# The softmax over positions in compensated fp32: one polynomial step made plain, and the reciprocal of the rational's denominator from two exponentials

## The chip, the cores and the metric

The kernel runs on one core of a Trainium2 chip. The metric is the device time of that core in microseconds (us): 1050.5 us for the kernel before, the median of three runs (1049.24, 1050.5 and 1057.09). The profile and the trace used below are of one further execution of 1053.18 us, whose span from the first to the last instruction is 1051.3 us at a mean granted TensorE clock of 0.805 of full speed. The engines are named as in the profile: PE (TensorE matmul), PEld (its weight load), DVE (VectorE), ACT (ScalarE), POOL (GpSimd) and SP (SyncE, which only issues DMA here).

## The reference

Two blocks follow each other. The first is an attention over 32 learned memory slots: `phi` is turned into weights by a softmax over the 576 positions, keys and values are pooled with these weights, and each query attends to the 32 pooled slots.

```python
# q, k, v: (8, 8, 576, 64); phi: (8, 8, 576, 32)
a = phi - np.max(phi, axis=2, keepdims=True)
a = np.exp(a)
a = a / (np.sum(a, axis=2, keepdims=True) + 1e-09)      # softmax over the positions
k_m = np.einsum('bhsm,bhsd->bhmd', a, k)
v_m = np.einsum('bhsm,bhsd->bhmd', a, v)
scores = scale * np.matmul(q, k_m.transpose(0, 1, 3, 2))
...                                                     # softmax over the 32 slots
out = np.matmul(attn, v_m)                              # -> x: (8, 576, 512)
```

The second is a mixture of depths: in each batch the 128 rows with the highest score `x @ w_gate` are replaced by `x + g * (relu(x @ w1) @ w2)`, where `g` is the sigmoid of the score; all other rows pass through.

```python
top_idx = np.argpartition(-scores[b], capacity)[:capacity]
xe = x[b, top_idx]
ye = np.maximum(xe @ w1, 0.0) @ w2
out[b, top_idx] = x[b, top_idx] + g[:, None] * ye
```

Which rows are chosen depends on the last bits of the scores. So the kernel computes the first softmax and the pooled values very close to fp32 rounding, in many VectorE steps.

## The kernel before, in words

**The work.** There are 16 *groups*: 8 batches times 2 halves of 4 heads. The phi of a group is one tile of 128 partitions (4 heads x 32 slots) by 576 positions. `softmax(i, ch)` turns it into weights, `keys(i, ch)` transposes them on PE, pools the keys and writes the weights in two parts (high and low bits) to DRAM. `split_v` splits the values into two parts and writes them to DRAM too. `values(st)` reads both back for two batches at a time and pools the values with 2304 small matmuls (L371). `attention(b)` is the second softmax, the output rows, the gate's scores, the ranking and the gather of the chosen rows; `ffn(b, t)` is the two-layer network on these rows.

**The softmax of a group.** All tiles are 128x576. The exponential is range reduced, exp(r) 2^q, and exp(r) is a rational: a numerator polynomial `num` with coefficients EXP_P and a denominator `den` with EXP_Q. Most Horner steps are done by `fma` (L216 to L225): six VectorE operations that multiply a value `val` by `r` with compensation, from its coarse part `h` (an int16 tile that ScalarE rounds, "vh" or "dh") and the coarse and fine parts `rh`, `rl` of `r`. It runs once for `den` (L229) and three times for `num` (L234 to L243). Then the quotient num/den is formed: `y0` is a first quotient in whole steps of a grid (an int16 tile from ScalarE's Exp, L233), `num - y0*den` is the remainder (L246 to L253), the reciprocal of `den` comes from a product of terms of ScalarE's Square (`sq` at L242, `s2` at L249, with L247 between them), and L257 to L259 multiply the remainder by it and add `y0`. L262 multiplies by 2^q and sums over the positions; L265 to L276 divide by the sum with compensation. ScalarE's part of all this goes through the helper `act` (L176).

**The order of the work.** The kernel schedules by hand. Every job is a generator, and the main loop (L747 on) is a list of *turns*: each turn takes one step of one softmax, some steps of `values`, one step of each live attention and two steps of the ffn queue. So a `yield` in `softmax` is a turn in which the other jobs get their share:

```python
if working and next(working[0], working) is working: ...     # one step of a softmax
if len(working) == 2 and turn % 2:
    next(working[1], None)                                    # split_v, every other turn
for _ in range(steps()):                                      # 7, 10 or 12 steps of values
    next(sums, None)
if attend_all is None and set(order[1]) <= set(made):
    finish(working.pop(1))                                    # what is left of split_v, at once
    ...                                                       # pools of the attention take its place
```

A softmax with its keys is 11 turns. Groups 0 to 7 are handled in two chains, `ex0` and `ex1`, whose steps alternate. When the odd groups are made, the pools of the second chain and of `split_v` are given up for the attention's tiles; groups 8 to 15 go through one chain, with the attentions between their steps. Each engine executes its own instructions in the order in which they were issued here.

Of the kernel before, what the change touches and what calls it, by code (L numbers as in the profile page):

```python
# [8 lines left out]
F32 = mybir.dt.float32  # L9
# [5 lines left out]
AF = mybir.ActivationFunctionType  # L15
ALU = mybir.AluOpType
# [8 lines left out]

LOG2E = 1.44269504088896341
LN2_HI, LN2_LO = 6.93145752e-1, 1.42860677e-6
EXP_P = (1.0, 7.257664613233124478488e-01, 2.473615434895520810817e-01,  # L30
         5.114512081637298353406e-02, 6.757896990527504603057e-03, 5.082762527590693718096e-04)
EXP_Q = (1.0, -2.742335390411667452936e-01, 2.159509375685829852307e-02)
EXP_LOWEST = -87.0
Y0_SCALE = 12 * 0.6931471805599453


@with_exitstack
def kernel(
# [61 lines left out]
    def load_k(i, ch):  # L100
        ks[i] = exs[ch].tile([PT, NC, D // NG], F32, name="kb")
        nc.sync.dma_start(out=ks[i], in_=k[groups[i]])
# [60 lines left out]
    def constant(value):  # L163
        t = const.tile([P, 1], F32, name=f"c{len(biases)}")
        nc.gpsimd.memset(t, value)
        return t


    UP, GRID = 2.0 ** 23, 2.0 ** -11
    biases = {}  # L170
    for x in (EXP_P[3] * UP, EXP_P[4] * UP, EXP_P[3] * UP * GRID, EXP_Q[1] * UP,
              EXP_Q[1] * UP * GRID, 127 * UP, -1.5, Y0_SCALE):
        biases[x] = constant(x)

    def act(dst, src, s=1.0, c=0.0, func=AF.Identity):
        nc.scalar.activation(dst, src, func, bias=biases[c] if c else 0.0, scale=s)  # L176

    tt, stt = nc.vector.tensor_tensor, nc.vector.scalar_tensor_tensor
# [3 lines left out]
    def softmax(i, ch):  # L182

        ex = exs[ch]

        def t(name, dtype=F32):

            return ex.tile([P, NC * P if name in WIDE else S], dtype, name=name)[:, :S]

        r = phis.pop(i)  # L190
        mx = ex.tile([P, 1], F32, name="mx")
        nc.vector.tensor_scalar(out=t("num"), in0=r, scalar1=1.0, scalar2=None, op0=ALU.mult,
                                op1=ALU.max, accum_out=mx)
        nc.vector.tensor_scalar(out=r, in0=r, scalar1=mx, scalar2=EXP_LOWEST,
                                op0=ALU.subtract, op1=ALU.max)
        q = t("q", I16)
        act(q, r, LOG2E)
        yield
        for ln2 in (LN2_HI, LN2_LO):
            stt(out=r, in0=q, scalar=-ln2, in1=r, op0=ALU.mult, op1=ALU.add)  # L200

        rh, rl = t("rh", I16), t("rl")
        act(rh, r, 2.0 ** 11)
        num, den = t("num"), t("den")
        act(num, r, EXP_P[5] * UP, EXP_P[4] * UP)
        dh = t("dh", I16)
        act(dh, r, EXP_Q[2] * UP * GRID, EXP_Q[1] * UP * GRID)
        act(den, r, EXP_Q[2] * UP, EXP_Q[1] * UP)
        yield
        tt(out=num, in0=num, in1=r, op=ALU.mult)  # L210
        vh = t("vh", I16)
        act(vh, num, GRID, EXP_P[3] * UP * GRID)
        act(num, num, 1.0, EXP_P[3] * UP)
        stt(out=rl, in0=rh, scalar=-GRID, in1=r, op0=ALU.mult, op1=ALU.add)

        def fma(val, h, c):  # L216


            lo, big, low = t("lo"), t("big"), t("low")
            stt(out=lo, in0=val, scalar=GRID, in1=h, op0=ALU.mult, op1=ALU.subtract)  # L220
            tt(out=lo, in0=lo, in1=rh, op=ALU.mult)  # L221
            tt(out=big, in0=h, in1=rh, op=ALU.mult)
            tt(out=low, in0=val, in1=rl, op=ALU.mult)
            tt(out=low, in0=low, in1=lo, op=ALU.add)  # L224
            stt(out=val, in0=big, scalar=c * UP, in1=low, op0=ALU.add, op1=ALU.add)  # L225

        yield
        load_k(i, ch)
        fma(den, dh, EXP_Q[0])  # L229
        dh = t("dh", I16)  # L230
        act(dh, den, GRID / 2)
        y0 = t("y0", I16)
        act(y0, r, 1.0, Y0_SCALE, AF.Exp)  # L233
        for c in (EXP_P[2], EXP_P[1], EXP_P[0]):  # L234
            yield
            fma(num, vh, c)
            if c != EXP_P[0]:
                vh = t("vh", I16)
                act(vh, num, GRID)
            if c == EXP_P[2]:  # L240
                sq = t("rl2")
                act(sq, den, 1.0 / UP, -1.5, AF.Square)  # L242


        dl, p = t("lo"), t("big")
        stt(out=dl, in0=den, scalar=GRID / 2, in1=dh, op0=ALU.mult, op1=ALU.subtract)  # L246
        stt(out=p, in0=sq, scalar=0.75, in1=den, op0=ALU.add, op1=ALU.mult)  # L247
        s2 = t("low")
        act(s2, p, 1.0 / UP, -1.5, AF.Square)  # L249
        tt(out=p, in0=y0, in1=dh, op=ALU.mult)  # L250
        tt(out=num, in0=num, in1=p, op=ALU.subtract)
        tt(out=dl, in0=y0, in1=dl, op=ALU.mult)
        tt(out=num, in0=num, in1=dl, op=ALU.subtract)  # L253
        two_q = t("den", I32)
        yield
        act(two_q, q, UP, 127 * UP)
        stt(out=num, in0=s2, scalar=0.75, in1=num, op0=ALU.add, op1=ALU.mult)  # L257
        stt(out=num, in0=sq, scalar=0.75, in1=num, op0=ALU.add, op1=ALU.mult)
        stt(out=num, in0=num, scalar=GRID, in1=y0, op0=ALU.mult, op1=ALU.add)  # L259
        sm = ex.tile([P, 4], F32, name="sm")  # L260
        e = t("e")
        stt(out=e, in0=num, scalar=GRID / 2, in1=two_q.bitcast(F32),  # L262
            op0=ALU.mult, op1=ALU.mult, accum_out=sm[:, 0:1])

        nc.vector.tensor_scalar_add(sm[:, 0:1], sm[:, 0:1], 1e-9)  # L265
        nc.vector.reciprocal(sm[:, 1:2], sm[:, 0:1])
        nc.vector.tensor_single_scalar(sm[:, 2:3].bitcast(I32), sm[:, 0:1].bitcast(I32), -4096,
                                       op=ALU.bitwise_and)
        nc.vector.tensor_sub(sm[:, 3:4], sm[:, 2:3], sm[:, 0:1])
        nc.vector.tensor_scalar_mul(sm[:, 2:3], sm[:, 2:3], -1.0)  # L270
        a0 = t("vh", F16)
        nc.scalar.activation(a0, e, AF.Copy, scale=sm[:, 1:2])
        yield
        for part in (2, 3):
            stt(out=e, in0=a0, scalar=sm[:, part:part + 1], in1=e, op0=ALU.mult, op1=ALU.add)
        stt(out=e, in0=e, scalar=sm[:, 1:2], in1=a0, op0=ALU.mult, op1=ALU.add)  # L276
        soft[i] = e
        yield
        yield from keys(i, ch)
# [28 lines left out]
    def keys(i, ch):  # L308
        ex, (b, g) = exs[ch], groups[i]
        a = soft.pop(i)  # L310
        kb = ks.pop(i)
        aS = ex.tile([P, NC * P], F32, name="lo")[:PT].rearrange("p (c m) -> p c m", m=P)
        for c0 in range(0, NC, 3):
            tp = bank([PT, 3, P])
            for c in range(3):
                nc.tensor.transpose(out=tp[:, c], in_=a[:, (c0 + c) * PT:(c0 + c + 1) * PT],  # L316
                                    identity=ident)
            nc.scalar.activation(aS[:, c0:c0 + 3], tp, AF.Copy)  # L318
        yield
        hi = ex.tile([P, NC * P], F32, name="big")[:PT].rearrange("p (c m) -> p c m", m=P)  # L320
        lo = ex.tile([P, NC * P], F32, name="low")[:PT].rearrange("p (c m) -> p c m", m=P)
        nc.vector.tensor_single_scalar(hi.bitcast(I32), aS.bitcast(I32), -4096,
                                       op=ALU.bitwise_and)
        nc.vector.tensor_sub(lo, aS, hi)  # L324
        for part, src in enumerate((lo, hi)):
            for h in range(4):
                nc.gpsimd.dma_start(  # L327
                    out=aparts[h, b, g, part].rearrange("(c p) m -> p c m", p=PT),
                    in_=src[:, :, h * M:(h + 1) * M])
        km = bank([P, 2, 2 * M])  # L330
        for rr in range(2):
            for c in range(NC):
                nc.tensor.matmul(out=km[:, rr], lhsT=kb[:, c, rr * P:(rr + 1) * P],  # L333
                                 rhs=aS[:, c, rr * 2 * M:(rr + 1) * 2 * M],
                                 start=(c == 0), stop=(c == NC - 1))
        for u in range(2):
            part = slice(u * Dh, (u + 1) * Dh)
            nc.scalar.activation(kbd[b][part, 2 * g:2 * g + 2, u * M:(u + 1) * M],
                                 km[part, :, u * M:(u + 1) * M], AF.Copy)
# [407 lines left out]
    while True:  # L747
# [27 lines left out]
        for _ in range(2):  # L775
# [8 lines left out]
                            op0=ALU.mult, op1=ALU.add)  # L784
# [42 lines left out]
```

## Time and profile before

| Stretch (us from the start) | What runs | DVE busy | PE busy | ACT busy | DMA share |
|---|---|---|---|---|---|
| 0 to 326.6 | groups 0 to 7 in two chains, splitting of v, values of the first two batches | 295.3 | 94.4 | 93.0 | 0.65 |
| 326.6 to 792 | groups 8 to 15 in one chain, attentions 0 to 3, values of batches 2 to 5 | 384.4 | 292.8 | 147.0 | 0.19 to 0.60 |
| 792 to 1051.3 | values of the last two batches, attentions 4 to 7, most of the ffns | 104.7 | 211.6 | 53.7 | 0.20 to 0.53 |

The stretches are cut at the start of a group's first VectorE instruction (L192; group 0 at 3.7, group 8 at 326.6, group 15 at 741.5) and shortly after the last instruction of the last softmax (L276, at 789.7). Each busy time is the sum of the durations on that engine within the stretch; a stretch in which an engine is busy nearly all of the time is bound by it. The busy times of the second and third stretch are sums over the groups' stretches of the same view.

Instructions of the softmax on 128x576 elements take close to the same time whatever they are: 742 to 885 ns on VectorE by the means of their groups, 681 to 776 ns on ScalarE. ScalarE loads its function tables once in the whole run (1283 ns).

### The profile page before, as it was taken

How to read it: one execution, taken by the hardware profiler on the slowest of the kernel's cores; microseconds unless marked ns; L12 is line 12 of the kernel's file. 1: busy time of each engine (PE TensorE's matmuls, PEld its weight loads, DVE VectorE, ACT ScalarE, POOL GpSimd, SP SyncE). 2: the span in 40 equal slices, each digit the busy share in tenths (PEclk: the TensorE clock that was granted, in tenths of full speed). 3: DMA queues.
4: the chain of work that ended last, by engine and by line, in shares of the span. 5: the costliest groups of instructions: out<-in, count | busy, mean ns of one | idle time of the engine just before them, and what ended most of it. 6: DMA issues, size and time to landing. Idle time of an engine off the chain costs nothing. (4 is left out here: it accounts for less than half of the span.)

```text
span 1051.3 us, 25384 instructions
## 1 busy us (share of the span) xinstructions
PE 598.7 (57%) x10738; PEld 439.8 (42%) x10738; DVE 784.4 (75%) x1342; ACT 293.6 (28%) x578; POOL 224.3 (21%) x335
## 2 busy tenths in 40 slices
PE   0021022255554355675567397875738969889795
PEld 0021022154443354554434374664415657544542
DVE  7899999899899968698786968698993336324940
ACT  2233233233233232323224342141432101213230
POOL 7030221220230230404113021402503011011110
PEclk9999999995665656877678699566866986989688
DMA  9364544677887825554613256463404466522320
GB/s 291 126 232 153 188 157 169 192 230 277 264 274 253 313 46 155 152 179 145 214 51 106 72 141 206 127 194 115 114 0 116 153 218 189 163 66 66 120 70 23
DMA packets 60714, 166.11 MB, mean 158 GB/s; under 512 B 10801, under 2 KB 21041, under 8 KB 60593
## 3 DMA queue, kind: packets, MB, share of 16 engines
q1 hardware_dynamic: 39088, 94.14, 29.5%
q0 software_dynamic: 21504, 70.27, 19.7%
q8 instruction: 87, 1.43, 0.6%
q14 instruction: 35, 0.28, 0.1%
HBM read 96.21 MB, written 68.16 MB: 156 GB/s over the span
## 5 line engine op out<-in xcount | busy, mean ns | idle before, releaser
L371 PE MATMUL acc<-a_rows,v_rows 32*64 32x128 f32 x9216 | 217.8, 257 | 106.7 <-DMA a_rows<-aparts 97.6
L371 PEld LDWEIGHTS acc<-a_rows,v_rows 32*64 32x64 f32 x9216 | 197.7, 167 | 150.2 <-issue 113.9
L316 PE MATMUL bank<-ident,e 128*96 128x128 f32 x96 | 22.5, 403 | 214.8 <-DVE e L276 204.6
L316 PEld LDWEIGHTS bank<-ident,e 128*96 128x96 f32 x96 | 16.0, 185 | 219.7 <-issue 183.4
L333 PE MATMUL bank<-lo,kb 96*128 96x64 f32 x384 | 67.0, 353 | 7.6 <-ACT lo L318 6.8
L333 PEld LDWEIGHTS bank<-lo,kb 96*128 96x128 f32 x384 | 65.5, 267 | 12.1 <-ACT lo L318 8.6
L327 POOL DMA_DIRECT2D aparts<-low x64 | 47.2, 746 | 104.5 <-DVE low L324 100.8
L646 PE MATMUL bank<-w_sb,hT 128*128 128x512 f32 x128 | 67.2, 661 | 0.0
L636 PE MATMUL bank<-w_sb,xeT 128*128 128x512 f32 x128 | 65.5, 647 | 2.9 <-ACT xeT L627 2.9
L530 PE MATMUL bank<-vbd,eT 128*128 128x256 f32 x160 | 60.0, 510 | 0.0
L221 DVE TENSOR_TENSOR lo<-lo,rh 128x576 f32<-128x576 f32 x64 | 56.7, 885 | 2.2
L176 ACT ACTIVATE vh<-num 128x576 int16<-128x576 f32 x32 | 21.8, 683 | 127.3 <-DVE num L225 116.7
L534 DVE TENSOR_TENSOR xj<-bank,rd 128x512 f32<-128x512 f32 x40 | 27.5, 688 | 36.8 <-PE bank L530 34.9
L537 POOL TENSOR_TENSOR xj<-xj,mean 128x1024 f32<-128x1024 f32 (+1 forms) x12 | 26.1, 2174 | 128.5 <-DVE xj L534 89.8
L583 DVE SCALAR_TENSOR_TENSOR cmp<-row,tg,wide 128x576 bf16<-128x576 f32 x40 | 32.5, 811 | 25.9 <-ACT row L569 25.1
L298 POOL DMA_DIRECT2D vparts<-vb x16 | 11.6, 726 | 186.2 <-DVE vb L295 161.9
L224 DVE TENSOR_TENSOR low<-low,lo 128x576 f32<-128x576 f32 x64 | 48.5, 758 | 2.2
L327 POOL DMA_DIRECT2D aparts<-big x64 | 46.7, 738 | 0.0
L220 DVE SCALAR_TENSOR_TENSOR lo<-num,vh 128x576 f32<-128x576 f32 x48 | 36.0, 751 | 13.2 <-ACT vh L176 13.2
L530 PEld LDWEIGHTS bank<-vbd,eT 128*128 128x128 f32 x160 | 35.0, 243 | 23.8 <-issue 19.6
L602 PE MATMUL bank<-tg,pick 128*128 128x2 f32 (+1 forms) x80 | 16.9, 329 | 47.4 <-DVE pick L597 20.2
L176 ACT ACTIVATE low<-big,c 128x576 f32<-128x576 f32 x16 | 12.4, 775 | 96.4 <-DVE big L247 96.4
(150 smaller groups left out, 1244.2 us busy)
## 6 DMA issues: line engine op xcount, KB each, us to landing
v_rows<-vparts SPq DMA_DIRECT2D x128, 288.0 KB
vparts<-vb POOLq DMA_DIRECT2D x16, 1152.0 KB, 5.2
vparts<-vhi POOLq DMA_DIRECT2D x16, 1152.0 KB, 8.9
a_rows<-aparts SPq DMA_DIRECT2D x512, 36.0 KB
vb<-in_v SPq DMA_DIRECT2D x16, 576.0 KB
kb<-in_k SPq DMA_DIRECT2D x16, 576.0 KB
qb<-in_qT SPq DMA_DIRECT2D x16, 576.0 KB
out<-xj POOLq DMA_DIRECT2D x16, 512.0 KB, 3.8
```

The costliest lines, as they stand in the source:

```text
L176: nc.scalar.activation(dst, src, func, bias=biases[c] if c else 0.0, scale=s)
L220: stt(out=lo, in0=val, scalar=GRID, in1=h, op0=ALU.mult, op1=ALU.subtract)
L221: tt(out=lo, in0=lo, in1=rh, op=ALU.mult)
L224: tt(out=low, in0=low, in1=lo, op=ALU.add)
L316: nc.tensor.transpose(out=tp[:, c], in_=a[:, (c0 + c) * PT:(c0 + c + 1) * PT], identity=ident)
L327: nc.gpsimd.dma_start(out=aparts[h, b, g, part].rearrange("(c p) m -> p c m", p=PT), in_=src[:, :, h * M:(h + 1) * M])
L333: nc.tensor.matmul(out=km[:, rr], lhsT=kb[:, c, rr * P:(rr + 1) * P], rhs=aS[:, c, rr * 2 * M:(rr + 1) * 2 * M], start=(c == 0), stop=(c = ...
L371: nc.tensor.matmul(out=accs[i][:Dh, :P].rearrange("p (h m) -> p h m", m=M), lhsT=vr[p, s], rhs=ar[p, :, s], start=(ch == 0 and s == 0), st ...
L530: nc.tensor.matmul(out=o[:, g * 4 * Dh:(g + 1) * 4 * Dh], lhsT=eT[:, g, (c0 + c) * P:(c0 + c + 1) * P], rhs=vbd[b % 3][:, g], start=False, ...
L583: nc.vector.scalar_tensor_tensor(out=cmp, in0=row, scalar=g, in1=wide[:, off:off + S], op0=ALU.is_equal, op1=ALU.mult, accum_out=equal[:, ...
L636: nc.tensor.matmul(out=ps[:n], lhsT=xeT[:, d, :n], rhs=w1_sb[:, d, f0:f0 + 512], start=(d == 0), stop=(d == KD - 1))
L646: nc.tensor.matmul(out=ps[:n], lhsT=hT[:, f, :n], rhs=w2_sb[:, f], start=(f == 0), stop=(f == KF - 1))
```

## The change

It shortens the arithmetic of `softmax` in three ways.

- One of the three compensated steps of the numerator becomes a plain fp32 one: a single multiply-add on VectorE in place of the six operations of `fma` and one rounding on ScalarE. The following coefficients move down by one.
- The reciprocal of the denominator is no longer built from two Squares and products on VectorE. ScalarE forms it straight from `r` as exp(exp(a r + b) + c), in two Exp instructions.
- `y0` is on a grid of 14 bits rather than 12, so that the remainder is smaller and needs a reciprocal of less accuracy. Two scalar_tensor_tensor that applied the two factors become one tensor_tensor, and the scaling by the grid moves into the last step.

Besides, the product `low` is the first operation of `fma` rather than the fourth, and a softmax has one `yield` less.

```diff
+INV = (0.11678339169584792, 0.8537669889679409, -2.34847734)
+LN2 = 0.6931471805599453
...
-    UP, GRID = 2.0 ** 23, 2.0 ** -11
+    UP, GRID, FINE = 2.0 ** 23, 2.0 ** -11, 2.0 ** -14
...
         tt(out=num, in0=num, in1=r, op=ALU.mult)
+        stt(out=num, in0=num, scalar=EXP_P[3] * UP, in1=r, op0=ALU.add, op1=ALU.mult)
         vh = t("vh", I16)
-        act(vh, num, GRID, EXP_P[3] * UP * GRID)
-        act(num, num, 1.0, EXP_P[3] * UP)
+        act(vh, num, GRID, EXP_P[2] * UP * GRID)
+        act(num, num, 1.0, EXP_P[2] * UP)
...
             lo, big, low = t("lo"), t("big"), t("low")
+            tt(out=low, in0=val, in1=rl, op=ALU.mult)
             stt(out=lo, in0=val, scalar=GRID, in1=h, op0=ALU.mult, op1=ALU.subtract)
             tt(out=lo, in0=lo, in1=rh, op=ALU.mult)
             tt(out=big, in0=h, in1=rh, op=ALU.mult)
-            tt(out=low, in0=val, in1=rl, op=ALU.mult)
             tt(out=low, in0=low, in1=lo, op=ALU.add)
...
-        act(dh, den, GRID / 2)
+        act(dh, den, FINE)
         y0 = t("y0", I16)
-        act(y0, r, 1.0, Y0_SCALE, AF.Exp)
-        for c in (EXP_P[2], EXP_P[1], EXP_P[0]):
+        act(y0, r, 1.0, 14 * LN2, AF.Exp)
+        inv = t("rl2")
+        act(inv, r, INV[0], INV[1], AF.Exp)
+        act(inv, inv, 1.0, INV[2] - 9 * LN2, AF.Exp)
+        for c in (EXP_P[1], EXP_P[0]):
             yield
             fma(num, vh, c)
             if c != EXP_P[0]:
                 vh = t("vh", I16)
                 act(vh, num, GRID)
-            if c == EXP_P[2]:
-                sq = t("rl2")
-                act(sq, den, 1.0 / UP, -1.5, AF.Square)
...
-        stt(out=dl, in0=den, scalar=GRID / 2, in1=dh, op0=ALU.mult, op1=ALU.subtract)
-        stt(out=p, in0=sq, scalar=0.75, in1=den, op0=ALU.add, op1=ALU.mult)
-        s2 = t("low")
-        act(s2, p, 1.0 / UP, -1.5, AF.Square)
+        stt(out=dl, in0=den, scalar=FINE, in1=dh, op0=ALU.mult, op1=ALU.subtract)
         tt(out=p, in0=y0, in1=dh, op=ALU.mult)
...
-        stt(out=num, in0=s2, scalar=0.75, in1=num, op0=ALU.add, op1=ALU.mult)
-        stt(out=num, in0=sq, scalar=0.75, in1=num, op0=ALU.add, op1=ALU.mult)
-        stt(out=num, in0=num, scalar=GRID, in1=y0, op0=ALU.mult, op1=ALU.add)
+        tt(out=num, in0=num, in1=inv, op=ALU.mult)
+        tt(out=num, in0=num, in1=y0, op=ALU.add)
...
-        stt(out=e, in0=num, scalar=GRID / 2, in1=two_q.bitcast(F32),
+        stt(out=e, in0=num, scalar=FINE, in1=two_q.bitcast(F32),
             op0=ALU.mult, op1=ALU.mult, accum_out=sm[:, 0:1])
```

## Prediction

> **What bounds the kernel now.** I read first the busy shares over time, then the busy times cut at the groups' starts, then VectorE's waits, then single instructions. The page's line of totals and three of its rows over 40 slices of 26.3 us:
>
> ```profile
> PE 598.7 (57%) x10738; PEld 439.8 (42%) x10738; DVE 784.4 (75%) x1342; ACT 293.6 (28%) x578; POOL 224.3 (21%) x335
> ...
> PE   0021022255554355675567397875738969889795
> DVE  7899999899899968698786968698993336324940
> DMA  9364544677887825554613256463404466522320
> ```
>
> VectorE's 75% is no average of alike stages: it is at 8 to 9 tenths up to slice 13, then mixed 6 to 9 up to slice 30, then 2 to 4 while PE takes over with 7 to 9. So there are three stages with different bounds, which the busy times in the stretches confirm (columns: stretch, length, busy us of PE, PEld, DVE, ACT, POOL, granted clock, DMA share, GB/s):
>
> ```profile
> 0.00:326.60 326.60, 94.36 (x2118) 86.99 (x2122) 295.30 (x429) 92.96 (x148) 78.80 (x133) 0.89 0.65 217
> ...
> 490.70:557.60 66.90, 43.56 (x779) 33.51 (x779) 55.27 (x102) 19.07 (x42) 16.82 (x21) 0.74 0.42 132
> ...
> 936.00:1051.30 115.30, 90.89 (x327) 48.45 (x326) 53.78 (x125) 29.91 (x73) 16.49 (x30) 0.84 0.20 66
> ```
>
> In the first stage DVE is busy 295 of 327 us and nothing else exceeds a third, except the DMA share of 0.65. In the second, 326.6 to 792 (eight such group stretches), DVE is busy 384 of 465 us (83%) and PE 293. In the tail, 792 to 1051, PE is busy 212 of 259 us. VectorE's waits over the whole run tell which of its gaps belong to the code that changes (columns: us in total, times, longest):
>
> ```profile
> DVE big L250 <- ACT low L176: 13.5, 16, 0.8
> DVE lo L220 <- ACT vh L176: 13.2, 18, 0.8
> DVE num L210 <- ACT num L176: 9.7, 5, 4.0
> ```
>
> The first two are small, but they recur in every group and both are of the changed code; up to 370 us all of its waits together are 25 us, 19.3 of them these two. Last, the order in time of one numerator step (start, us):
>
> ```profile
> 346.97 0.75 DVE L220 SCALAR_TENSOR_TENSOR lo<-num,vh 128x576 f32<-128x576 f32 x1
> ...
> 350.68 0.76 DVE L225 SCALAR_TENSOR_TENSOR num<-big,low 128x576 f32<-128x576 f32 x1
> 352.19 0.76 DVE L220 SCALAR_TENSOR_TENSOR lo<-num,vh 128x576 f32<-128x576 f32 x1 [0.75 <-ACT vh L176]
> ```
>
> One `fma` is 4.4 us of instructions, set 0.67 to 0.79 us apart from start to start, plus 0.8 us of waiting for ScalarE's rounding where nothing of another job stands between.
>
> **What the Trainium skill says.** "VectorE: DVE Perf Modes", section on the TRN2 errata, gives (N+151)/0.96 ns for an fp32 tensor_tensor: 757 ns at N = 576. The trace has 750 to 758, so no form in the diff is cheaper than another and only the count matters. "ScalarE: Activation LUTs", "What ACT_TABLE_LOAD costs", gives 280 + 0.833 N ns for an ACTIVATE with a pointer bias, whatever the function: 760 ns here; the Exp of `y0` is 761 and the Square 760 in the trace. The same page, "Table sets: the hidden batching unit", says that only a change of table set costs a load. The trace has one load (1283 ns) though Exp, Square, Tanh and Sign alternate, and the changed program has one too, so two more Exps cost no load.
>
> **The change part by part.** Per group, VectorE:
> - One `fma` goes: -4.4 us. L247 goes: -0.68. L257 to L259 become two operations: -0.8. One multiply-add comes: +0.75. Net -5.1 us of path; 43 instructions on 128x576 become 36.
> - The wait of L250 for `s2` goes, since neither new Exp waits for VectorE: -0.84.
> - The two waits of L220 for `vh` shrink: one goes with its `fma`, the other is covered because `low` (0.67 us) is now issued ahead and needs no `vh`. Of these 11.7 us lie before 370 us, over eight groups 1.46 each; I take 0.2 as what remains.
> - ScalarE: two Squares and a rounding go (760 + 775 + 683 ns), two Exps come (2 x 760). They stand behind `dh` and `y0`, while VectorE does the next `fma` (4.4 us); ScalarE is 28% busy. What queues behind them is the `vh` of that `fma`, needed later. Cost nothing.
>
> A `yield` less shifts the interleaving: a group takes 10 turns rather than 11, the main loop 224 rather than 240. Following the built program's order:
> - *New waits in the first stage.* L210 waits for ScalarE's `rh` and `num`. Before, 2.2 us or more of the other chain's work lay between in all groups but the first (which waited 1.41 us). Now nothing lies between in five more of the first nine: +1.4 us each, 7 in all. The keys' L322 also comes sooner behind ScalarE: +0.5 in six groups, 3 in all. Behind both, VectorE's whole queue is held.
> - *The end of split_v.* It advances every other turn, but the first eight groups now end at turn 83, not 92. So two groups of v are finished in one turn instead of one. The last load can only start once an earlier write (5.2 us to landing by the page, 9.6 at most) has freed its buffer; then it must arrive ahead of L293, which blocks VectorE. I put 6 us of write, 3 of issue and 4 of load against some 6 us of VectorE work between: a stall of 8 us; ends 0 and 20.
> - *Work pushed into the tail.* With fewer turns, less attention and ffn stands ahead of the last softmax. Counting instructions: VectorE loses 16 us of attention from the second stage (one ranking of five L583 at 0.81, and neighbours). PE loses 25 us: 14 of the 128 ffn matmuls of L636 and L646 at about 1.03 us each with their passes, and the rest scores and transposes. Both come back in the tail.
>
> Sums. First stage: 8 x 5.1 = 41, plus waits 8 x (0.84 + 1.46 - 0.2) = 17, less new waits 10: -48 us. End of split_v: +8. Second stage: 41 + 16 moved + 8 of waits = 65 us off VectorE. But PE is 63% busy there and VectorE's gaps are partly PE's doing (L534 waits 15.5 us for it in this stage), so I take 85%: -55; ends -33 (half) and -65. Tail: the 25 us on an engine that is 82% busy, of which idle time absorbs a little: +20; ends +5 and +30. Together -75 us: 1050.5 - 75 = 975.5, so 975.
>
> **Rivals.**
> - *DMA and PE take part of it back.* For it: the share of 0.65 over 326 us becomes about 0.76 over 279, and from 197 to 345 us, where the values are read back, it is 0.76 at 256 GB/s already and would go to about 0.9. PE waited 50 us there for a_rows. A late transpose would hold L322. Against: PE also waited 31.6 us for VectorE's `e` there, which is slack. First stage -38, split_v +12, second stage -40, tail +25: -41, or 1010.
> - *More than forecast.* The moved work falls into PE's idle time (48 us of the tail) and VectorE's saving passes through whole: -48 + 0 - 65 + 5 = -108, or 942. Against: the tail's PE gaps are mostly short.
> - *Slower.* The first stage becomes bound by transfers and gains nothing, split_v stalls VectorE for 30 us, half of the second stage's gain arrives, and the tail takes 30: 30 - 33 + 30 = +27, about 1078. Against: VectorE did not wait for a single vb load before, and the DMA share has slices at 9.
>
> **How the numbers follow.** Forecast (965 to 990): 0.55. Partly taken back (990 to 1039): 0.22. More (below 965): 0.18. Slower or no change: 0.05. The range goes from 945, just above the sum of the good ends, to 1008, inside the second case; what I leave out is a little of both. Faster by over 1% is thus 0.95, within 1% 0.02, slower 0.03.
>
> **What the profile after would show.** DVE some 85 us less busy; 688 softmax instructions of 128x576 turned into 576. Group 8's first L192 (326.6 before) near 280 and the last softmax near 697. No L250 wait and next to none at the first operations of `fma`; longer waits of the num multiply (L210) for ScalarE, about 1.4 us each. A wait of L293's successor for a vb load near the end of the first stage. A tail of about 280 us from the last softmax, PE at over 80%. I would be wrong if the DMA share of the first stage stood at 0.9 with VectorE waiting, if a second table load appeared, or if the tail grew by far more than 20 us.

## The result, and the profile after

The changed kernel takes 975.9 us (median of four runs, 973.72 to 977.07) against 1049.87 before: a ratio of 0.9285, 95% interval 0.9233 to 0.9338. The page of its profile, the line of totals and the rows over 40 slices (24.4 us each now):

```profile
PE 599.5 (61%) x10738; PEld 440.2 (45%) x10738; DVE 706.3 (72%) x1231; ACT 285.4 (29%) x562; POOL 228.2 (23%) x335
...
PE   0022103446762266677874969677888887789795
DVE  7999999998981987868999686979734323455930
...
DMA  8464756598789554656570556654346455221410
```

VectorE is 78 us less busy for 112 instructions fewer in the program (85 us were forecast), PE as busy as before. The shape is the same, three stages that are now shorter, shorter and longer. One thing is new: the "1" in slice 13 of the DVE row, in a stretch in which VectorE was never below 8 before. Busy times in the three stages and in that hole (columns: stretch, length, busy us of PE, PEld, DVE, ACT, POOL, granted clock, DMA share, GB/s):

```profile
0.00:279.70 279.70, 89.97 (x1862) 82.73 (x1866) 256.02 (x381) 88.71 (x142) 77.29 (x132) 0.86 0.70 233
...
290.00:318.00 28.00, 9.54 (x356) 8.98 (x348) 5.86 (x7) 1.22 (x3) 9.12 (x13) 0.68 0.94 327
279.70:692.00 412.30, 278.44 (x5932) 213.83 (x5926) 329.81 (x580) 133.02 (x268) 106.13 (x131) 0.73 0.55 167
692.00:975.20 283.20, 231.11 (x2957) 143.64 (x2955) 120.46 (x272) 63.64 (x154) 44.77 (x72) 0.85 0.37 113
```

In the hole VectorE works 5.9 of 28 us, and the transfers run at a share of 0.94 and 327 GB/s. VectorE's waits name it (us in total, times, longest):

```profile
DVE vhi L292 <- DMA vb<-in_v: 11.9, 1, 11.9
DVE num L213 <- ACT num L179: 10.7, 8, 1.4
DVE vhi L292 <- DMA aparts<-big: 10.2, 1, 10.2
...
DVE lo L225 <- ACT vh L179: 4.1, 2, 3.0
```

The wait for `s2` (13.5 us before) is gone, the 18 waits for `vh` (13.2 us) are two, the multiply of `num` (L213, L210 before) waits more often, and there are 22.1 us of waits at L292, the first operation of the splitting of v, where there were none. VectorE's instructions in order of time (start, us) show both sides. First a compensated step right behind another:

```profile
325.23 0.76 DVE L229 SCALAR_TENSOR_TENSOR num<-big,low 128x576 f32<-128x576 f32 x1
326.02 0.76 DVE L224 TENSOR_TENSOR low<-num,rl 128x576 f32<-128x576 f32 x1
326.74 0.76 DVE L225 SCALAR_TENSOR_TENSOR lo<-num,vh 128x576 f32<-128x576 f32 x1
```

The product `low` starts 0.79 us after the L229 before it, and L225, which needs ScalarE's `vh`, follows 0.72 us later without a wait. Then the end of the splitting of v:

```profile
289.95 0.95 DVE L323 TENSOR_TENSOR low<-lo,big 96x768 f32<-96x768 f32 x1
301.07 0.76 DVE L292 TENSOR_SCALAR vhi<-vb 128x1152 int32<-128x1152 int32 x1 [10.16 <-DMA aparts<-big]
301.86 1.36 DVE L294 TENSOR_TENSOR vb<-vb,vhi 128x1152 f32<-128x1152 f32 x1
315.12 0.76 DVE L292 TENSOR_SCALAR vhi<-vb 128x1152 int32<-128x1152 int32 x1 [11.91 <-DMA vb<-in_v]
```

Two groups of v are finished in one turn, and VectorE stands still ahead of each. The issues of SyncE (start, us) tell why already the first is late:

```profile
292.35 0.50 SPq L349 DMA_DIRECT2D v_rows<-vparts  x1
292.90 2.45 SPq L356 DMA_DIRECT2D a_rows<-aparts  x4
295.45 0.58 SPq L284 DMA_DIRECT2D vb<-in_v  x1
...
305.84 0.33 SPq L284 DMA_DIRECT2D vb<-in_v  x1
```

The load that VectorE needed at 291 was issued at 295.45, behind the read-back of the values in the same queue. The profile names another transfer for this wait (`aparts<-big`). But L292 waits for two things here, its load and an earlier write from the buffer that it fills, and that write had landed at 281.51; so by exclusion it is the load.

The next load was issued at 305.84, and VectorE started on it 9.3 us later. Its buffer had to be freed first by a write, whose place in POOL's queue explains a part of the delay (a wait of SyncE between 268 and 312 us, then POOL's issues in time):

```profile
SPq L284 <- DMA vparts<-vb: 5.9, 1, 5.9
...
291.20 0.77 POOL L326 DMA_DIRECT2D aparts<-low  x1 [20.82 <-DVE low L323]
...
294.56 2.90 POOL L326 DMA_DIRECT2D aparts<-big  x4
297.45 0.71 POOL L297 DMA_DIRECT2D vparts<-vb  x1
```

The data of this write were ready at 286.97, the end of L294 for the group of v before these two. POOL issued it only at 297.45, after the eight writes of the keys' weights, the first of which waited for VectorE. It landed at 305.79.

### The profile page after: what moved, and what is told of

Read it like the earlier page. It is cut to its first block, busy times and chain, and to the rows that moved or that the text cites. A ratio compares the mean times of both kernels' runs of the same rounds, so it can differ in the third digit from the quotient of the medians.

```text
span 975.2 us, 25239 instructions
## 1 busy us (share of the span) xinstructions
PE 599.5 (61%) x10738; PEld 440.2 (45%) x10738; DVE 706.3 (72%) x1231; ACT 285.4 (29%) x562; POOL 228.2 (23%) x335
## 4 chain that ended last, share of the span: by engine, by line
PE 23%; DVE 23%; DMA 6%; SPq 4%; issue 3%; ACT 2%; POOL 1%; DVEq 0%; POOLq 0%
PE bank L645 5%; PE acc L370 5%; PE bank L635 4%; SPq L356 3%; DMA a_rows<-aparts 3%; PE bank L529 3%; DMA xe<-xs,idx 2%; DVE lo L225 1%; DVE low L224 1%; PE bank L332 1%; DVE big L227 1%; DVE four L503 1%; DVE low L228 1%; DVE prod L501 1%; PE bank L516 1%
## 5 line engine op out<-in xcount | busy, mean ns | idle before, releaser
L635 PE MATMUL bank<-w_sb,xeT 128*128 128x512 f32 x128 | 70.8, 689 | 5.2 <-ACT xeT L626 5.2
L645 PE MATMUL bank<-w_sb,hT 128*128 128x512 f32 x128 | 63.3, 627 | 0.0
L529 PE MATMUL bank<-vbd,eT 128*128 128x256 f32 x160 | 62.2, 526 | 0.0
L536 POOL TENSOR_TENSOR xj<-xj,mean 128x1024 f32<-128x1024 f32 (+1 forms) x11 | 25.5, 2316 | 119.9 <-DVE xj L533 100.9
L635 PEld LDWEIGHTS bank<-w_sb,xeT 128*128 128x128 f32 x128 | 26.0, 218 | 30.6 <-issue 22.0
L226 DVE TENSOR_TENSOR lo<-lo,rh 128x576 f32<-128x576 f32 x48 | 36.4, 758 | 1.6
L521 DVE TENSOR_SCALAR rd<-bank 128x16 f32<-128x16 f32 (+1 forms) x24 | 4.0, 166 | 45.8 <-PE bank L516 45.8
L271 ACT ACTIVATE vh<-e,sm 128x576 f16<-128x576 f32 x16 | 12.4, 775 | 84.5 <-DVE sm L266 84.5
L460 DVE SCALAR_TENSOR_TENSOR eT<-es,th 128x288 f32<-128x288 f32 x32 | 14.4, 450 | 30.2 <-ACT th L458 30.1
L228 DVE TENSOR_TENSOR low<-low,lo 128x576 f32<-128x576 f32 x48 | 36.0, 751 | 0.0
```

Source lines behind the costliest of these rows:

```text
L529: nc.tensor.matmul(out=o[:, g * 4 * Dh:(g + 1) * 4 * Dh], lhsT=eT[:, g, (c0 + c) * P:(c0 + c + 1) * P], rhs=vbd[b % 3][:, g], start=False, ...
L635: nc.tensor.matmul(out=ps[:n], lhsT=xeT[:, d, :n], rhs=w1_sb[:, d, f0:f0 + 512], start=(d == 0), stop=(d == KD - 1))
L645: nc.tensor.matmul(out=ps[:n], lhsT=hT[:, f, :n], rhs=w2_sb[:, f], start=(f == 0), stop=(f == KF - 1))
```

## The experiments

Cut in the same way for every kernel, in us: the first stage ends at the first operation of group 8, the second at the end of the last softmax. The last column is the second stage and the tail together, less the waits for v that fall into them. The stages are of the profiled run, the time is the median.

Three things limit how finely the stages can be compared. A profiled run is one execution, and some lie off their median: by 7 us for the old arithmetic in ten turns (1087.57 against 1080.4), by 10 us for the splitting taken forward (968.95 against 959.2). Of the 16 splittings of v, about 2 us of VectorE each, 14 lie ahead of group 8 in the kernel before and at eleven turns, 13 at ten turns, 15 at twelve and with the splitting taken forward. And in three of the profiled runs (the turn put back, and the two runs of one part alone) the first compensated step starts some 3 us sooner. There the second instruction of the first softmax takes about 2 us; in all other runs, the kernel before among them, it takes over 10 us while POOL clears tiles. The changed kernel, then the turn put back:

```profile
4.50 10.24 DVE L197 TENSOR_SCALAR ph<-ph,mx 128x576 f32<-128x576 f32 x1
...
4.47 2.12 DVE L197 TENSOR_SCALAR ph<-ph,mx 128x576 f32<-128x576 f32 x1
```

In the other groups this instruction (L194 in the kernel before) takes 0.52 us, by the median; it is thus outside the range of 742 to 885 ns given for the softmax. No edit touches it, so these 3 us are not counted for any.

| Kernel | time | first | second | of it waits for v | tail | second + tail, less waits |
|---|---|---|---|---|---|---|
| before (eleven turns) | 1050 | 326.6 | 463.9 | 0 | 260.8 | 724.7 |
| old arithmetic, ten turns | 1080.4 | 340.9 | 459.8 | 20.3 | 285.1 | 724.6 |
| changed kernel (ten turns) | 975.9 | 279.7 | 409.0 | 22.1 | 286.5 | 673.4 |
| new arithmetic, eleven turns | 956.3 | 272.4 | 419.1 | 0.9 | 264.7 | 682.9 |
| changed kernel, splitting taken forward | 959.2 | 289.8 | 394.1 | 0 | 283.3 | 677.4 |
| new arithmetic, twelve turns | 976.9 | 290.7 | 429.9 | 8.3 | 249.2 | 670.8 |

**The turn put back.**

```diff
                 act(vh, num, GRID)
-
+        yield
         dl, p = t("lo"), t("big")
```

> The changed kernel with the eleventh turn of a softmax put back (a bare yield ahead of the quotient's remainder), so that the new arithmetic runs under the old interleaving. Theory 1 (VectorE's path in the first two stages sets the time, and the missing turn itself costs): against the changed kernel (975) the stall at the end of the splitting (22 us) goes, some 10 us of new waits in the first stage go, and the tail loses its 26 us of growth, while the second stage takes back about 16 us of attention work: about 930. Rival (transfers and PE bind once VectorE is shorter): the gain is given back elsewhere, 960 to 980. Second rival (fewer turns are in themselves a gain, less interleaving): slower than 980.

956.3 us, ratio to before 0.9097 (0.9014 to 0.9181), so some 20 us faster than the changed kernel. The stall is gone but for 0.9 us in the second stage, and so is the growth of the tail (286.5 to 264.7). But the second stage came out at 419, where 409.0 - 22.1 + 16 = 403 was expected. The first stage is 7 us shorter, 3 of them from the start described above. The expected 930 was missed, and it was not the rival's 960 to 980 either. The turn stands in another place here than in the kernel before, ahead of the remainder and not among the numerator's steps, so the number of turns is the old one and the order is not quite.

**The turn taken from the old arithmetic.**

```diff
         for c in (EXP_P[2], EXP_P[1], EXP_P[0]):
-            yield
+            if c != EXP_P[2]:
+                yield
             fma(num, vh, c)
```

> The kernel before with one yield fewer per softmax (the first numerator step joins the denominator's), so that the old arithmetic runs in ten turns. Theory 1: the missing turn costs by itself: new waits in the first stage 10, two groups of v split at once 10 to 20, tail +26, second stage -16: about 1075 to 1090. Rival (the turn costs nothing, the small waits and the tail are absorbed): 1045 to 1055.

1080.4 us, ratio 1.0265 (1.0183 to 1.0347): a turn less costs by itself about 30 us (19 to 36 by the interval), and this was as expected. Only this one place was tried for the turn that goes. The waits of VectorE in it, in its first stage and then in its second:

```profile
DVE num L210 <- ACT num L176: 8.5, 6, 1.4
...
DVE big L323 <- ACT lo L319: 4.3, 7, 0.8
```

```profile
DVE vhi L294 <- DMA vb<-in_v: 20.3, 2, 13.9
```

The wait for ScalarE's `num` comes six times and not once, up to 1.4 us each; the keys wait seven times for ScalarE, which copies their transposes; and the two waits for v are there with the old arithmetic too. The tail grew by 24.3 us, and the second stage shrank by 4.1 + 20.3 = 24.4 us when its waits for v are taken out. The last column of the table is 724.7 and 724.6: what moves into the tail is taken off the second stage, as nearly as two single runs can show. What moves can be seen from the windows behind the last softmax: from the kernel before to this run VectorE's instructions there go from 236 to 275 and its busy time from 105 to 124 us, PE's busy time from 213 to 236 us.

**The splitting taken forward.** The changed kernel, with

```diff
-        if len(working) == 2 and turn % 2:
+        if len(working) == 2 and (turn % 2 or turn % 10 == 0):
```

> The changed kernel with the splitting of v taken forward in every tenth turn besides the odd ones, so that it is done before the odd groups are made and nothing of it is left for one burst. Theory 1 (the 22 us stall of VectorE is the burst's: a write, a load and VectorE in sequence): 950 to 958, with no VectorE wait for vb. Rival (the transfers of the first stage are the bound, the DMA share was 0.94 in the stall): the wait moves to other instructions, 968 to 978.

959.2 us, ratio 0.9093 (0.8998 to 0.9188). The two long waits are gone; one wait for a vb load is left, in the first stage:

```profile
DVE vhi L292 <- DMA vb<-in_v: 5.1, 1, 5.1
```

The time is 1 us above what was expected and below the rival's. So ten turns without the burst are as fast as eleven turns, within what can be told here (0.9093 and 0.9097), although the work that moved stays in the tail (283.3). The burst is thus most of the difference between the changed kernel and the eleven turns: 17 of the 20 us by the medians.

**One part alone: the plain step**, the reciprocal from Squares and eleven turns kept (a bare yield ahead of the remainder replaces the one that goes with the step, and the first Square follows the first step that is left; neither is in the lines shown):

```diff
         tt(out=num, in0=num, in1=r, op=ALU.mult)
+        stt(out=num, in0=num, scalar=EXP_P[3] * UP, in1=r, op0=ALU.add, op1=ALU.mult)
...
-        for c in (EXP_P[2], EXP_P[1], EXP_P[0]):
+        for c in (EXP_P[1], EXP_P[0]):
```

> The kernel before with the plain multiply-add in place of one compensated step alone, the reciprocal from Squares kept and eleven turns kept. Theory 1: VectorE's path is shorter by 4.4 - 0.75 = 3.65 us per group and by a wait of 0.8 where it was not hidden: 16 x 3.65 + 8 x 0.75 = 64, so about 985. Rival (half of the second stage's gain is lost to PE): about 1000 to 1015.

993.5 us, ratio 0.9459 (0.9381 to 0.9538): 57 us less, halfway between theory 1 (64) and the nearest end of the rival (50). The interval, 49 to 65 us, takes in both. A wait of 5.7 us for a load of v stands at the end of the splitting here too.

**The other part alone: the reciprocal**, the changed kernel without the plain step, which has eleven turns by its three steps:

```diff
-        stt(out=num, in0=num, scalar=EXP_P[3] * UP, in1=r, op0=ALU.add, op1=ALU.mult)
...
-        for c in (EXP_P[1], EXP_P[0]):
+        for c in (EXP_P[2], EXP_P[1], EXP_P[0]):
```

> The other part alone: the reciprocal from two Exps, the 14-bit grid and the earlier product low, but all three compensated steps of the numerator and eleven turns. Theory 1 (each operation on VectorE's path counts, the parts add): two operations fewer, 0.68 + 0.8 = 1.5 us per group, the wait for the second Square (0.84) gone, and some 1.5 us per group of waits for vh covered in the first stage: 16 x 2.3 + 8 x 1.5 = 49, so about 1000; together with the plain step alone (993.5, -57) this gives the -94 of the two at eleven turns (956), so by that difference about 1013. Rival (this part is only what it leaves out in instructions, 16 x 1.5 = 24): 1026.

1006.4 us against 1051.7 beside it, ratio 0.9579 (0.951 to 0.9647): 45 us, well over the 24 of its two instructions and between the 49 and the 37 that theory 1 came to in its two ways. The other 21 us fit the waits: the 13.5 us for `s2` are gone, and of the 13.2 us at the operations that need `vh` these are left:

```profile
DVE lo L224 <- ACT vh L179: 5.0, 2, 3.7
...
DVE low L223 <- ACT vh L179: 0.4, 1, 0.4
```

So the waits that go count about as much as the instructions; the earlier place of `low` belongs to this part. The two parts give 57 + 45 = 102 us, both together at eleven turns gave 94; each of these numbers is good to some 8 us, so they add as far as can be told.

**The place of `low`**, put back to the fourth operation:

```diff
-            tt(out=low, in0=val, in1=rl, op=ALU.mult)
             stt(out=lo, in0=val, scalar=GRID, in1=h, op0=ALU.mult, op1=ALU.subtract)
             tt(out=lo, in0=lo, in1=rh, op=ALU.mult)
             tt(out=big, in0=h, in1=rh, op=ALU.mult)
+            tt(out=low, in0=val, in1=rl, op=ALU.mult)
```

> The changed kernel with the product low put back to the fourth place of the compensated step. Theory 1 (its place covers ScalarE's rounding, one wait of 0.7 to 0.8 us per group in the first stage and some in the second): +6 to +12, so 982 to 988, with the first operation of the step waiting for vh again. Rival (the wait is absorbed by the transfers' stall or by PE): 974 to 978.

979.6 us, ratio 0.9293 (0.9228 to 0.9359). The wait is back, now at L224:

```profile
DVE lo L224 <- ACT vh L179: 9.8, 9, 2.7
```

The first stage is 5.1 us longer (284.8). The time is 3.7 us above the changed kernel's, below the expected 982 to 988 and above the rival's, and the two intervals lie over each other: what the earlier product gains in total could not be told.

**The two Exps done twice**, 1.5 us more of ScalarE per group:

```diff
         act(inv, r, INV[0], INV[1], AF.Exp)
         act(inv, inv, 1.0, INV[2] - 9 * LN2, AF.Exp)
+        act(inv, r, INV[0], INV[1], AF.Exp)
+        act(inv, inv, 1.0, INV[2] - 9 * LN2, AF.Exp)
```

> The changed kernel with the two new Exps done twice over on ScalarE (1.5 us more per group, 24 in all). Theory 1 (ScalarE's work here lies beside a compensated step of 4.4 us): 974 to 984, at most a short wait of VectorE for vh where ScalarE is late. Rival (ScalarE is on the path, every Exp counts): about 1000.

976.3 us, ratio 0.9245 (0.9162 to 0.9327). ScalarE's groups show the doubled instructions (count, busy us, mean ns, idle before):

```profile
L179 ACT ACTIVATE rl<-rl,c 128x576 f32<-128x576 f32 x32 | 24.8, 776 | 1.0
L179 ACT ACTIVATE rl<-ph,c 128x576 f32<-128x576 f32 x32 | 24.6, 768 | 0.5
...
L179 ACT ACT_TABLE_LOAD x1 | 1.3, 1283 | 0.7 <-PEq L813 0.7
```

ScalarE is busy 310.2 us, 24.8 more, and the time is that of the changed kernel. The Exps lie beside the compensated step, and there is one table load.

**A third buffer for the splitting of v:**

```diff
-    vio = first.enter_context(tc.tile_pool(name="vio", bufs=2))
+    vio = first.enter_context(tc.tile_pool(name="vio", bufs=3))
```

> The changed kernel with three buffers rather than two for the splitting of v, so that the last load needs no earlier write. Theory 1 (the stall is the sequence write, load, VectorE): the second wait for vb shrinks from 11.9 us to about 6, 968 to 972. Rival (the transfers are saturated in this stretch, DMA share 0.94, and both loads come late whatever frees their buffers): the stall stays about 22 us, 974 to 978.

970.7 us, ratio 0.92 (0.9128 to 0.9272). Both waits remain:

```profile
DVE vhi L292 <- DMA vb<-in_v: 15.9, 2, 10.7
```

The first is 10.7 us as before (10.2), the second 5.2 us where it was 11.9: theory 1 was right on the second, whose load no longer needs the earlier write, and the time fell within its range, though the interval overlaps that of the changed kernel. The first stays, as the rival has it for both: its load is late in the queue, in a stretch of 0.89 DMA share (290 to 320 us of this run).

**Twelve turns**, the eleven and one bare yield more within the remainder:

```diff
         tt(out=num, in0=num, in1=p, op=ALU.subtract)
+        yield
         tt(out=dl, in0=y0, in1=dl, op=ALU.mult)
```

> The changed kernel with two bare yields more, so twelve turns per softmax. Theory 1 (once the splitting leaves no burst, turns only move attention and ffn work between the second stage and the tail, and what one loses the other gains): about 950 to 962, like eleven turns (956.3), with a shorter tail and a longer second stage. Rival (PE's idle time ahead of the tail is worth filling, each turn gains the tail's 22 us): 930 to 940.

976.9 us, ratio 0.927 (0.9228 to 0.9311), outside both expectations. The second stage and the tail together lose nothing (670.8 in the last column against 682.9). The loss is in the first stage, 18 us longer than with eleven turns. Some 3 of these are the start described above and 2 are one splitting of v more; VectorE's waits up to 282 us show the rest:

```profile
DVE e L262 <- ACT den L179: 13.7, 7, 2.0
DVE vhi L293 <- DMA vb<-in_v: 9.0, 2, 4.6
```

At this offset of the two chains ScalarE's last conversion comes late for L262 in seven cases, and the splitting waits for its loads. A turn moves the distances between ScalarE's results and their readers, and here to the worse.

**ScalarE's `num` issued ahead of its rounding `rh`**, at eleven turns:

```diff
-        act(rh, r, 2.0 ** 11)
         num, den = t("num"), t("den")
         act(num, r, EXP_P[5] * UP, EXP_P[4] * UP)
+        act(rh, r, 2.0 ** 11)
```

> The changed kernel at eleven turns, with ScalarE's affine step for num issued ahead of its rounding rh. VectorE's multiply of num waits for this step, with the rounding (0.68 us) in front of it. Theory 1 (VectorE's path counts): the waits of that multiply, 14.8 us in the changed kernel at eleven turns, shrink by about a third, 950 to 955 against 956.3. Rival (they are absorbed): 956.

958.7 us, ratio 0.9092 (0.9055 to 0.9128), no gain over 956.3. The waits for `num` fell from 14.8 to 6.9 us, and the stages are 274.6, 420.1 and 260.3. But 5.6 of these 7.9 us are the first group's wait, 6.5 us after the short start and 0.9 us after a long one, and for the most part not the edit's: after the changed kernel's long start it is 1.4 us. The other groups' waits fell only from 8.3 to 6.0 us, which is too little to be seen in the time.

The fastest version is the new arithmetic at eleven turns, 956.3 us; the ones with the splitting taken forward and with `num` ahead of `rh` are not to be told from it.

## Why the prediction was right, point by point

**The cost of the change on VectorE's path: right.** -48 us were forecast for the first stage and group 8 near 280; it starts at 279.7, against 326.6 (2 of the 46.9 us are a splitting of v that now falls behind this point). The busy time there fell by 39 us where 8 x 5.1 = 41 were forecast, and the waits in all by 8 where it was 7. The two runs of one part alone add up to the whole within what can be told.

**The new waits in the first stage: right in one half.** L213 waits six times before 279.7 us, 8.5 us in all; before, one such wait of 1.4 us stood there, and the forecast added 7. The 3 us at the keys' L321 did not come there; in the old arithmetic with ten turns they did (4.3 us).

**The Exps cost nothing: right**, shown by doing them twice. The Trainium skill ("ScalarE: Activation LUTs", "What ACT_TABLE_LOAD costs") gives 760 ns by its formula for 576 elements; the two Exps measured 760 and 776 in the changed kernel.

**The end of split_v: right in kind, mis-sized.** 8 us with ends 0 and 20 were forecast; it is 22.1, beyond the far end. The step that failed took the first of the two loads as arrived; it stood behind the read-back of the values in SyncE's queue, and VectorE waited 10.2 us for it. For the last load 6 us of write, 3 of issue and 4 of load were put, 13 in all. From the issue of the write to its landing it took 8.3 us, the load was issued at once, and VectorE started 9.3 us after that; the write itself was late in POOL's queue. Both loads ran in a stretch of 327 GB/s.

**The moved work: the step that was thought wrongly.** The sum took 85% of 65 us off the second stage and put 20 us on the tail, as if what VectorE loses and what PE gains were two prices. The amount was counted nearly right: 16 us of VectorE and 25 of PE were forecast to move, and behind the last softmax VectorE is 18 and PE 21 us busier. Measured without the stall, the second stage lost 463.9 - (409.0 - 22.1) = 77 us and the tail gained 25.7. The old arithmetic with ten turns shows what this is: one transfer, 24 us off the one and 24 us onto the other. With the moved work out, the new arithmetic takes about 51 us from the second stage and tail together at ten turns (724.6 to 673.4) and 42 at eleven (724.7 to 682.9); 41 + 8 = 49 was the forecast of its parts, and the 15% taken off for PE were not needed. Why eleven turns got 9 us less is not settled; a part may be that the run of the old arithmetic in ten turns lies 7 us above its median.

**The sum was close because errors met.** The stall cost 14 us more than the forecast and the tail 6 more, the second stage gave 22 more: 975 against 975.9. That these cancel to 1 us is luck. The last softmax ended at 688.8, where 697 was forecast.

**The rivals.** Half of the first came true in place: the transfers did hold VectorE, in one stretch of 28 us and not over the stage, and PE did not hold the second stage back (it lost 77 us, more than the 65 that were counted for VectorE). The second, the large gain of 942, is not reached by any version: its best would need the tail nearly unchanged with all of the moved work gone from the second stage, and these exclude each other. The eleven turns (956.3) are the nearest. Of the third, the slower kernel, the stall was the only part that came near its size (22 of 30 us); VectorE's saving came through in both stages.

## What to carry to other kernels

In a kernel whose jobs are interleaved by hand, a yield is part of the price of an edit: take the order of the built program and ask for every wait what still stands between the producer and its reader, and for every job that is flushed at a stage's end how much of it is left. Work that only moves from one stage to the next is one number with two signs: here 24 us in ten turns, with no cost in the sum. What cost was the splitting that fell into one burst, a sequence of load, compute and write that nothing overlapped. Count the small recurring waits as well as the instructions: here they were, by the difference of the sums, about half of what the new reciprocal gave. And a profiled run has accidents of its own (here 3 us at the start, and 7 to 10 us off the median), so a reading of a few us from one trace each is not a finding.

## What was not expected of the hardware

A load of 576 KB issued at 305.84 us, into a stretch in which the DMA engines were busy 0.94 of the time at 327 GB/s, let VectorE start on it at 315.12, over 9 us later. Before the change the same load was issued at 332.8 and used at 344.9 without a wait, since 12 us lay between.

A stall of VectorE need not show as idle time. In the second stage, before (at 443 us) as after, instructions of 0.2 to 1 us are recorded as up to 3 us long while POOL computes at L537 (L536 after; start, us):

```profile
443.05 2.74 POOL L537 TENSOR_TENSOR xj<-xj,mean 128x1024 f32<-128x1024 f32 x1 [7.65 <-DVE xj L534]
...
443.60 2.81 DVE L221 TENSOR_TENSOR lo<-lo,rh 128x576 f32<-128x576 f32 x1
```

L221 takes 758 ns by its median. The excess over the medians adds up to 15 us in the second stage before and 16 after, which counts as busy time and stands in no list of waits.
